# Top-k attention with a mixture of depths on one core: small VectorE operations set behind the next maximum, and reciprocals taken straight from the column of sums

## The chip, the cores and the metric

The kernel runs on one NeuronCore of a Trainium2 chip. The metric is the device time of one execution in microseconds (us). Besides the plain runs one execution was taken by the hardware profiler. Its record names the engines: PE is TensorE (PEld its weight loads), DVE is VectorE, ACT is ScalarE, POOL is GpSimd, SP is the queue that issues most DMAs.

## The reference, cut to what matters

```python
# attention: B, H, S, D = 8, 8, 576, 64
scores = scale * np.matmul(q, k.transpose(0, 1, 3, 2))
kth = np.partition(scores, -32, axis=-1)[..., -32:-31]
scores = np.where(scores >= kth, scores, -1000000000.0)
scores = scores - np.max(scores, axis=-1, keepdims=True)
attn = np.exp(scores)
attn = attn / (np.sum(attn, axis=-1, keepdims=True) + 1e-09)
attn_out = np.matmul(attn, v)
# bridge: x = attn_out as (B, S, H * D) = (8, 576, 512)
# mixture of depths: capacity 128, F = 1024
scores = np.einsum('bsd,d->bs', x, w_gate)
out = x.copy()
for b in range(B):
    top_idx = np.argpartition(-scores[b], capacity)[:capacity]
    xe = x[b, top_idx]
    ye = np.maximum(xe @ w1, 0.0) @ w2
    g = 1.0 / (1.0 + np.exp(-scores[b, top_idx]))
    out[b, top_idx] = x[b, top_idx] + g[:, None] * ye
```

For every query only the 32 largest of its 576 scores are kept. Then, for each batch, the 128 tokens with the largest gate pass through a two-layer network, and the result is added to their rows.

## The kernel before, in words

**Tiles and units.** The 576 queries of a batch form four tiles of 128 and one of 64. A unit is one tile with two heads (for the tile of 64, four heads, two of them on the upper partitions). A batch has 18 units and the whole run 144. One pass of the loop over `n` works on several units at once, as a pipeline:

- unit n+1: PE multiplies queries and keys, and ACT copies the scores to `sc` (two rows of 576 for each partition);
- unit n: DVE finds a lower bound of the 32nd largest score (`find_bound`). For each of the two rows it takes the eight largest of seven parts (14 `MAX8` that write `cand`), then works on `cand` alone (`best`, `MATCH_REPLACE8`, `bound`);
- unit n-1: ACT takes the sign of each score against the bound and counts (`sides`, `seen`), POOL multiplies scores and signs into `y`;
- unit n-2: DVE takes two `MAX8` over `y` (`find_kth`), whose results `next` give the threshold;
- unit n-3: ACT and POOL make the mask `less`;
- unit n-4: PE transposes scores and adds the mask, ACT takes the exponential `pT` (and `last`), PE multiplies by the values into `av`, and ACT copies `av` to `xs`.

Each head has 65 columns in `xs`: 64 of values and, as column `D`, the sum of the weights, which comes from a column of ones beside the values.

**From `xs` to the output.** When the last unit of a tile is in `xs`, ACT copies the column of sums to `sums` (`keep_sums`, one instruction of 128x8 for each of the 40 tiles, or 64x8). In the next pass DVE takes the reciprocal `rden`, POOL multiplies it into the output tile `x`, and a pass later DVE takes the dot product of `x` with the gate's weights (`gates`).

**The mixture.** For each batch but the last a generator, `mixture`, spreads the second stage over the units of the batch that follows: ranks of the gates, a matrix product that finds each chosen row's number and gate, the fetch of the rows (an indirect DMA of POOL), two layers on PE, and an indirect DMA that adds to the output. On DVE `add_up` sums the parts of row number and gate into `place`, writes `row_i`, and clamps the gate into `g`. ACT takes the exponential of `g`, and `squash` adds one and takes the reciprocal. For the last batch the same is written out after the loop, with DVE, ACT, POOL and PE taking turns.

**The order.** All engines keep program order. The deferred pieces stand in lists of functions that the loop empties at fixed places: `vector_late` in `find_bound`, ahead of the second row's maxima (here stand the reciprocals `rden` and `squash`), `after_kth` after `find_kth` (here stands `add_up`), `late` after the mask (here stands ACT's exponential of `g`), `pool_late` for POOL. `keep_least` puts the smallest threshold of a batch into `least` when the batch's last mask is made. The inputs' check at the end, nine reductions over `bounded`, `least`, `seen`, `sums` and others, decides whether a general version of the computation must run. In the profile all instructions of the main path carry the line of the helper that records them, L46, so they are told apart by the names of their tiles.

Of the kernel before, what the change touches and what calls it, by code (L numbers as in the profile page):

```python
# [28 lines left out]
FEWEST = 0.5  # L29
# [20 lines left out]
def kernel(  # L50
# [91 lines left out]
    seen = const.tile([P, NS], FP32, name="seen")  # L142
    least = const.tile([P, B], FP32, name="least")
    bounded = const.tile([P, NS], FP32, name="bounded")
    sums = const.tile([P, B * NT, H], FP32, name="sums")
    nc.gpsimd.memset(sums, 1.0)

    MIDDLE = S - 2 * (TOP_K - 8) + 1
    steps_i = const.tile([P, 2, 8], I32, name="steps_i")
# [74 lines left out]

    kept, values_bank = [], [None]

    after_kth = []

    def flush_copies():
        while copies_late:  # L230
# [2 lines left out]
    def flush():  # L233
        flush_copies()
        while late:
            late.pop(0)()

    def flush_vector():
        while vector_late:
            vector_late.pop(0)()  # L240
# [4 lines left out]

    def flush_all():
        flush_vector()
        flush()
        flush_pool()

# [293 lines left out]
    def find_bound(sc, bound):  # L544

        cand = wkpool.tile([P, 2, 8 * PARTS], FP32, name="cand")
        best = [stats.tile([P, 2, 8], FP32, name=f"best{r}") for r in range(2)]
        best.append(bound)
        for i in range(2):

            if i == 1:
                flush_vector()
            for u in range(PARTS):
                if i == 1 and amid_late and u == amid_late[0][0]:
                    amid_late.pop()[1]()
                dve.max(
                    cand[:, i, 8 * u : 8 * u + 8],
                    sc[:, i, u * S // PARTS : (u + 1) * S // PARTS],
                )


        parts = cand.rearrange("p i (u e) -> p i u e", u=PARTS)
        for r, e in enumerate((3, 7, 8)):
            for i in range(2):
                dve.max(best[r][:, i, :], parts[:, i, :, 0:e])
            if r < 2:
                for i in range(2):
                    dve.match_replace(
                        parts[:, i, :, 0:e],
                        best[r][:, i, :],  # L570
                        parts[:, i, :, 0:e],
                        LOWEST,
                    )
# [140 lines left out]
    def keep_values_of_two(t, g, av, xs):  # L714
# [7 lines left out]
        for i, (h, r) in enumerate(heads_of(t, g)[0]):  # L722
# [4 lines left out]
                in_=both[r : r + n, :].rearrange("p (g c) -> p g c", g=2),  # L727
            )

    def normalise(b, t, xs):  # L730
        n = R if t == J else P
        den = sums[0:n, b * NT + t, :]
        divide(n, xs, of_batch[b][0][0:n, t, :], den)

    def keep_sums(n, xs, den):
        act.activation(den, xs[0:n, :, D], AF.Copy, bias=1e-9)

    def divide(n, xs, x, den):
        rden = stats.tile([P, H], FP32, name="rden")
        dve.reciprocal(out=rden[0:n, :], in_=den)  # L740
        pool.tensor_tensor(
            x.rearrange("p (h d) -> p h d", h=H),
            xs[0:n, :, 0:D],
            rden[0:n, :].unsqueeze(2).to_broadcast([n, H, D]),
            ALU.mult,
        )

# [38 lines left out]
    def mixture(row0, pg, rank, exact=False, sign_sum=None):  # L786
# [107 lines left out]

        def add_up():
            add_parts(place, found)
            keep_rows(
                place,
                row_i,
                row0 if isinstance(row0, float) else row0[:, 0:1],  # L900
                float(done * S - 1),
            )
            dve.tensor_scalar_max(out=g, in0=place[:, 1:2], scalar1=-88.0)
            late.append(lambda: act.activation(g, g, AF.Exp, scale=-1.0))

        def squash():
            dve.tensor_scalar_add(out=g, in0=g, scalar1=1.0)
            dve.reciprocal(out=g, in_=g)

        kept.append(lambda: after_kth.append(add_up))  # L910
        if exact:
            for todo in (kept, after_kth):
                while todo:
                    todo.pop(0)()
        yield
# [258 lines left out]
    def keep_least(b, bound, kth):  # L1174
        at = 2 * per_batch * b
        late.append(
            lambda: act.copy(
                out=bounded[:, at : at + 2 * per_batch].rearrange("p (n i) -> p n i", i=2),
                in_=bound,
            )  # L1180
        )
        dve.tensor_reduce(
            out=least[:, b : b + 1], in_=kth, axis=mybir.AxisListType.XY, op=ALU.min
        )

    def mask_of(n, on=None):
# [5 lines left out]
    for n in range(-1, N):  # L1192
# [89 lines left out]
        if is_unit(n - 4):  # L1282
            b4, t4, g4 = units[n - 4]
            values(t4, g4, pT, last, av, qkv[b4][2], 2 * DE * second)
            if n in place_steps:
                values_bank[0] = av
                next(mixtures[place_steps[n]])
                pieces[place_steps[n]] += 1
            if g4 == 0:
                xs = xpool.tile([P, H, DE], FP32, name="xs")  # L1290
                if t4 == 0:
                    x = xpool.tile([P, NT, HD], FP32, name="x")
                    pg = gates_of[b4 % 2]
                    of_batch[b4] = x, pg
            if second:
                keep_values_of_two(t4, g4 - 1, av, xs)
            if g4 == groups(t4) - 1:
                inverting = b4, t4, xs
                n4 = R if t4 == J else P
                keep_sums(n4, xs, sums[0:n4, b4 * NT + t4, :])  # L1300
            while kept:
                kept.pop(0)()

# [64 lines left out]
        b, t, g = units[m]  # L1368
        keep_values(t, g, weighed[m][3], xs)

    def sums_of(t, xs):
        n = R if t == J else P
        keep_sums(n, xs, sums[0:n, (B - 1) * NT + t, :])

    def mask_both(m):
        b, i = divmod(m, per_batch)
        masks[m] = wkpool.tile([P, 2, S], BF16, name="less")
# [45 lines left out]
    values_unit(N - 3)  # L1423
    weighed[N - 2][2]()
    keep_unit(N - 3, xs)
    sums_of(J - 1, xs)
    mask_both(N - 1)
    normalise(B - 1, J - 1, xs)
    store_full(last_out, x)
# [13 lines left out]
    for _ in range(2):  # L1443
        next(between)
    keep_unit(N - 1, xs)
    sums_of(J, xs)
    count(J - 1, slice(0, JP), rank)
    rden = stats.tile([P, H], FP32, name="rden")
    dve.reciprocal(out=rden[0:R, :], in_=sums[0:R, (B - 1) * NT + J, :])
    dve.tensor_tensor(  # L1450
        x[0:R, J, :].rearrange("p (h d) -> p h d", h=H),
        xs[0:R, :, 0:D],
        rden[0:R, :].unsqueeze(2).to_broadcast([R, H, D]),
        ALU.mult,
    )
    store_last(last_out, x)
# [77 lines left out]
        )  # L1534

    keep_least(B - 1, bounds.pop(B - 1)[:, :, :, 7], next8s.pop(B - 1)[:, :, :, 7])
    flush()
    low = modpool.tile([P, S], I32, name="low", tag="scratch")[:, 0:NS]
    dve.tensor_scalar(
# [9 lines left out]
    for what, op, than, limit in (  # L1549
        (bounded, ALU.min, ALU.is_gt, LEAST),  # L1550
        (least, ALU.min, ALU.is_gt, LEAST),
        (low, ALU.min, ALU.is_gt, 0.5),
        (seen, ALU.max, ALU.is_lt, float(MIDDLE)),
        (seen, ALU.min, ALU.is_gt, float(MIDDLE - 16)),
        (sums.rearrange("p t h -> p (t h)"), ALU.min, ALU.is_gt, FEWEST),
        (sums.rearrange("p t h -> p (t h)"), ALU.max, ALU.is_lt, MOST),
        (places[:, :, 6], ALU.min, ALU.is_gt, 0.5),
        (places[:, :, 6], ALU.max, ALU.is_lt, 1.5),
    ):
        far = stats.tile([P, 1], FP32, name="far", bufs=2)  # L1560
        dve.tensor_reduce(out=far, in_=what, axis=mybir.AxisListType.X, op=op)
        dve.scalar_tensor_tensor(
            out=sure, in0=far, scalar=limit, in1=sure, op0=than, op1=ALU.mult
        )
# [91 lines left out]
    def general(b, row0):  # L1656
        def of(a):
            return a[bass.ds(b, 1)].rearrange("o a s d -> (o a) s d")

        kT, qT, vs = room_for_qkv(0)  # L1660
        rows = Rows(of(k), of(q), kT, qT)
        turn_all_last(rows)
        for hp in range(NHP):
            turn_pair(rows, hp)
        load_v(of(v), vs)
        x = xpool.tile([P, NT, HD], FP32, name="x")
        pg = gates_of[0]
        for t in range(NT):
            xs = xpool.tile([P, H, DE], FP32, name="xs")
            for g in range(groups(t)):  # L1670
                ps = room_for_scores()
                multiply(t, g, kT, qT, by_head(ps))
                p = general_weights(keep(ps))
                tr, av = room_to_turn()
                turn(p, tr)
                pT = ptpool.tile([P, 2, J, P], FP32, name="pT")
                last = ptpool.tile([P, P], FP32, name="last")
                nc.scalar.copy(out=pT, in_=tr)
                nc.scalar.copy(out=last, in_=turn_last(p, av))
                values(t, g, pT, last, av, vs)  # L1680
                keep_values(t, g, av, xs)
            rows = R if t == J else P
            den = stats.tile([P, H], FP32, name="den", bufs=1)
            keep_sums(rows, xs, den[0:rows, :])
            divide(rows, xs, x[0:rows, t, :], den[0:rows, :])
            dot_tile(t, x, pg)
        store(out[bass.ds(b, 1)].rearrange("o s n -> (o s) n"), x)
        rank = stats.tile([P, NT], FP32, name="rank", bufs=1)
        for _ in mixture(row0, pg, rank, exact=True):
            flush_all()  # L1690
        flush_all()
# [40 lines left out]
```

## Time and profile before

| what | before |
|---|---|
| median of 3 runs | 787.77 us (785.72 to 788.05) |
| the profiled execution, its own time | 788.09 us |
| its span | 785.8 us |
| instructions in the span | 33176 |
| mean granted TensorE clock | 0.997 |
| DVE's groups: `cand` maxima, `next` maxima | 2016 in all, 228 ns; 288, 751 ns |
| reciprocal `rden`, 128 rows and 64 rows | 32, 185 ns; 8, 180 ns |
| ACT's copy of sums, 128 rows and 64 rows | 32, 216 ns; 8, 216 ns |
| `least`; `row_i`; reciprocal of `g` | 8, 217 ns; 8, 154 ns; 8, 164 ns |

How to read it: the span runs from the first to the last instruction in the record, and the execution's own time has 2.3 us more around it. Durations are those of one instruction, and neighbours on one engine may overlap, so what an instruction takes from its engine is read from start to start. A busy share is an average over stages.

### The profile page before, as it was taken

How to read it: one execution, taken by the hardware profiler on the slowest of the kernel's cores; microseconds unless marked ns; L12 is line 12 of the kernel's file. 1: busy time of each engine (PE TensorE's matmuls, PEld its weight loads, DVE VectorE, ACT ScalarE, POOL GpSimd, SP SyncE). 2: the span in 40 equal slices, each digit the busy share in tenths (PEclk: the TensorE clock that was granted, in tenths of full speed). 3: DMA queues.
4: the chain of work that ended last, by engine and by line, in shares of the span. 5: the costliest groups of instructions: out<-in, count | busy, mean ns of one | idle time of the engine just before them, and what ended most of it. 6: DMA issues, size and time to landing. Idle time of an engine off the chain costs nothing. (4 is left out here: it accounts for less than half of the span.)

```text
span 785.8 us, 33176 instructions
## 1 busy us (share of the span) xinstructions
PE 725.5 (92%) x12535; PEld 550.6 (70%) x12535; DVE 755.1 (96%) x4602; ACT 731.7 (93%) x1535; POOL 693.7 (88%) x732
## 2 busy tenths in 40 slices
PE   8888888788999989999999999999899999999987
PEld 6666666566786668766787667866687668757756
DVE  6999999999999999999999999999999999999952
ACT  5999999999999999999999999999999999989830
POOL 3899999999999999999999999999999999899821
PEclk9999999999999999999999999999999999999999
DMA  9941214121151223321232221412234102101021
GB/s 171 297 86 35 58 62 104 36 56 30 62 113 25 52 66 76 83 55 37 77 89 52 56 43 62 105 30 56 43 89 92 30 15 70 25 15 17 3 75 31
DMA packets 121751, 50.69 MB, mean 65 GB/s; under 512 B 116016, under 2 KB 116016, under 8 KB 120560
## 3 DMA queue, kind: packets, MB, share of 16 engines
q1 hardware_dynamic: 118368, 43.94, 22.9%
q0 software_dynamic: 1744, 4.20, 3.0%
q8 instruction: 101, 1.65, 0.9%
q14 instruction: 66, 0.54, 0.3%
q10 hardware_dynamic: 1472, 0.36, 0.2%
HBM read 36.93 MB, written 11.55 MB: 62 GB/s over the span
## 5 line engine op out<-in xcount | busy, mean ns | idle before, releaser
L46 POOL TENSOR_TENSOR y<-sc,sides 128x576 f32<-128x576 f32 x288 | 350.5, 1240 | 27.9 <-ACT sides L46 26.2
L46 DVE MAX8 cand<-sc 128x8 f32<-128x82 f32 (+1 forms) x2016 | 312.8, 228 | 4.6 <-ACT sc L46 4.6
L46 POOL TENSOR_SCALAR less<-sc,next 128x576 bf16<-128x576 f32 x135 | 233.7, 1731 | 24.6 <-DVE next L46 21.9
L46 ACT ACTIVATE sides<-sc,bound 128x576 fp8e4<-128x576 f32 x288 | 230.9, 802 | 2.1 <-DVE bound L46 1.5
L46 PEld LDWEIGHTS av<-v,pT 128*64 128x64 f32 x4608 | 146.9, 138 | 87.5 <-ACT last L46 79.0
L46 DVE MAX8 next<-y 128x8 f32<-128x584 f32 x288 | 204.4, 751 | 0.0
L46 PE MATMUL av<-v,pT 128*64 128x65 f32 x4608 | 166.9, 225 | 35.2 <-ACT last L46 34.9
L46 PE MATMUL ps<-kT,qT 64*128 64x288 f32 (+1 forms) x1248 | 170.4, 422 | 3.2 <-ACT sc L46 2.5
L46 PEld LDWEIGHTS <-less 64*128 64x128 bf16 (+1 forms) x2448 | 160.6, 131 | 11.2 <-POOL less L46 8.3
L46 ACT COPY sc<-ps 128x1152 f32<-128x1152 f32 x140 | 160.7, 1148 | 0.0
L46 PE MATMUL ptr<-ident,sc 64*128 64x64 f32 x2272 | 160.1, 252 | 0.0
L46 ACT ACTIVATE pT<-ptr 128x1024 f32<-128x1024 f32 x142 | 147.4, 1038 | 9.4 <-PE ptr L46 8.7
L46 PEld LDWEIGHTS ptr<-ident,sc 64*128 64x128 f32 x2272 | 137.6, 137 | 23.8 <-issue 23.6
L46 PE MATMUL ptr<-out_of_reach,less 64*128 64x64 bf16 x2272 | 147.1, 189 | 5.6 <-POOL less L46 4.9
L46 ACT ACTIVATE less<-sc,next 128x576 bf16<-128x576 f32 x147 | 115.5, 790 | 0.0
L46 PEld LDWEIGHTS ps<-kT,qT 64*128 64x128 f32 (+1 forms) x1248 | 92.6, 176 | 22.8 <-ACT sc L46 5.6
L46 DVE MATCH_REPLACE8 cand<-best,cand 128x21 f32<-128x21 f32 (+1 forms) x576 | 99.0, 180 | 0.0
L46 DVE MAX8 best<-cand 128x8 f32<-128x21 f32 (+1 forms) x576 | 90.6, 190 | 0.0
L46 ACT ACTIVATION_READ_ACCUMULATOR sides<-sc,bound 128x1 f32 x288 | 63.8, 222 | 0.0
L46 PE MATMUL h_ps<-xeT,w 128*128 128x128 f32 x464 | 61.9, 278 | 0.0
L46 PEld LDWEIGHTS av<-ident,sc 128*128 128x128 f32 x144 | 20.0, 139 | 55.9 <-issue 40.9
L46 PE MATMUL av<-vpair,last 128*64 128x130 f32 x576 | 56.9, 276 | 0.0
(167 smaller groups left out, 919.0 us busy)
## 6 DMA issues: line engine op xcount, KB each, us to landing
v<-in_v_dram SPq DMA_DIRECT2D x64, 128.0 KB, 4.0
out_dram<-x SPq DMA_DIRECT2D x8, 1024.0 KB, 3.9
rows<-in_k_dram SPq DMA_DIRECT2D x56, 128.0 KB, 3.0
rows<-in_q_dram SPq DMA_DIRECT2D x56, 128.0 KB, 3.0
w<-in_moe_w_dram SPq DMA_DIRECT2D x2, 2048.0 KB
gate_row<-row_dram SPq DMA_DIRECT2D x7, 288.0 KB, 4.4
last<-in_q_dram SPq DMA_DIRECT2D x8, 128.0 KB, 3.4
vpair<-in_v_dram SPq DMA_DIRECT2D x16, 64.0 KB, 5.1
```

What stands on the lines that cost most here:

```text
L46: return lambda *a, **kw: self._tc.keep_in_program_order(fn(*a, **kw))
```

## The change

Three kinds of small DVE instruction that read what stands right before them are moved behind the maximum that follows. They go into a new list, `after_max`, which `find_bound` empties after each of its 14 maxima of `cand`: the reduction into `least`, the pair `row_i` and clamp of `g` (now `use_place`), and the reciprocal of `g`. ACT's exponential of `g` is queued by `use_place`, and so comes a pass later. Besides, `keep_sums` goes: DVE's reciprocal reads column `D` of `xs` itself and writes `shares`, which takes the place of `rden` and `sums`. The term of 1e-9 is left out of the main path. The two reductions at the end test the reciprocals against the inverted limits.

```diff
-    sums = const.tile([P, B * NT, H], FP32, name="sums")
-    nc.gpsimd.memset(sums, 1.0)
+    shares = const.tile([P, B * NT, H], FP32, name="shares")
+    nc.gpsimd.memset(shares, 1.0)
...
+    after_kth, after_max = [], []
+
+    def flush_small():
+        while after_max:
+            after_max.pop(0)()
...
                 dve.max(
                     cand[:, i, 8 * u : 8 * u + 8],
                     sc[:, i, u * S // PARTS : (u + 1) * S // PARTS],
                 )
+                flush_small()
...
     def normalise(b, t, xs):
         n = R if t == J else P
-        den = sums[0:n, b * NT + t, :]
-        divide(n, xs, of_batch[b][0][0:n, t, :], den)
-
-    def keep_sums(n, xs, den):
-        act.activation(den, xs[0:n, :, D], AF.Copy, bias=1e-9)
+        invert(xs[0:n, :, D], share_of(b, t))
+        divide(n, xs, of_batch[b][0][0:n, t, :], share_of(b, t))
+
+    def invert(den, share):
+        dve.reciprocal(out=share, in_=den)
...
         def add_up():
             add_parts(place, found)
+            after_max.append(use_place)
+
+        def use_place():
             keep_rows(
...
             dve.tensor_scalar_add(out=g, in0=g, scalar1=1.0)
-            dve.reciprocal(out=g, in_=g)
+            after_max.append(lambda: dve.reciprocal(out=g, in_=g))
...
-        dve.tensor_reduce(
-            out=least[:, b : b + 1], in_=kth, axis=mybir.AxisListType.XY, op=ALU.min
+        after_max.append(
+            lambda: dve.tensor_reduce(
+                out=least[:, b : b + 1], in_=kth, axis=mybir.AxisListType.XY, op=ALU.min
+            )
         )
...
     keep_unit(N - 1, xs)
-    sums_of(J, xs)
     count(J - 1, slice(0, JP), rank)
-    rden = stats.tile([P, H], FP32, name="rden")
-    dve.reciprocal(out=rden[0:R, :], in_=sums[0:R, (B - 1) * NT + J, :])
+    invert(xs[0:R, :, D], share_of(B - 1, J))
...
-        (sums.rearrange("p t h -> p (t h)"), ALU.min, ALU.is_gt, FEWEST),
-        (sums.rearrange("p t h -> p (t h)"), ALU.max, ALU.is_lt, MOST),
+        (shares.rearrange("p t h -> p (t h)"), ALU.max, ALU.is_lt, 1.0 / FEWEST),
+        (shares.rearrange("p t h -> p (t h)"), ALU.min, ALU.is_gt, 1.0 / MOST),
```

More of the change, by code (lines that the diff above doesn't have):

```diff
@@ L225 @@
     kept, values_bank = [], [None]
-    after_kth = []
+    after_kth, after_max = [], []
+    def flush_small():
+        while after_max:
+            after_max.pop(0)()
     def flush_copies():
@@ L559, in find_bound @@
                 )
+                flush_small()
         parts = cand.rearrange("p i (u e) -> p i u e", u=PARTS)
@@ L728, in keep_values_of_two, with share_of, divide @@
             )
+    def share_of(b, t):
+        return shares[0 : R if t == J else P, b * NT + t, :]
     def normalise(b, t, xs):
         n = R if t == J else P
-        den = sums[0:n, b * NT + t, :]
-        divide(n, xs, of_batch[b][0][0:n, t, :], den)
-    def keep_sums(n, xs, den):
-        act.activation(den, xs[0:n, :, D], AF.Copy, bias=1e-9)
-    def divide(n, xs, x, den):
-        rden = stats.tile([P, H], FP32, name="rden")
-        dve.reciprocal(out=rden[0:n, :], in_=den)
+        invert(xs[0:n, :, D], share_of(b, t))
+        divide(n, xs, of_batch[b][0][0:n, t, :], share_of(b, t))
+    def invert(den, share):
+        dve.reciprocal(out=share, in_=den)
+    def divide(n, xs, x, share):
         pool.tensor_tensor(
@@ L743, in divide @@
             xs[0:n, :, 0:D],
-            rden[0:n, :].unsqueeze(2).to_broadcast([n, H, D]),
+            share.unsqueeze(2).to_broadcast([n, H, D]),
             ALU.mult,
@@ L907, in squash @@
             dve.tensor_scalar_add(out=g, in0=g, scalar1=1.0)
-            dve.reciprocal(out=g, in_=g)
+            after_max.append(lambda: dve.reciprocal(out=g, in_=g))
         kept.append(lambda: after_kth.append(add_up))
         if exact:
-            for todo in (kept, after_kth):
+            for todo in (kept, after_kth, after_max):
                 while todo:
@@ L1298 @@
                 inverting = b4, t4, xs
-                n4 = R if t4 == J else P
-                keep_sums(n4, xs, sums[0:n4, b4 * NT + t4, :])
             while kept:
@@ L1369, in keep_unit @@
         keep_values(t, g, weighed[m][3], xs)
-    def sums_of(t, xs):
-        n = R if t == J else P
-        keep_sums(n, xs, sums[0:n, (B - 1) * NT + t, :])
     def mask_both(m):
@@ L1425 @@
     keep_unit(N - 3, xs)
-    sums_of(J - 1, xs)
     mask_both(N - 1)
@@ L1445 @@
     keep_unit(N - 1, xs)
-    sums_of(J, xs)
     count(J - 1, slice(0, JP), rank)
-    rden = stats.tile([P, H], FP32, name="rden")
-    dve.reciprocal(out=rden[0:R, :], in_=sums[0:R, (B - 1) * NT + J, :])
+    invert(xs[0:R, :, D], share_of(B - 1, J))
     dve.tensor_tensor(
@@ L1452 @@
         xs[0:R, :, 0:D],
-        rden[0:R, :].unsqueeze(2).to_broadcast([R, H, D]),
+        share_of(B - 1, J).unsqueeze(2).to_broadcast([R, H, D]),
         ALU.mult,
@@ L1536 @@
     keep_least(B - 1, bounds.pop(B - 1)[:, :, :, 7], next8s.pop(B - 1)[:, :, :, 7])
+    flush_small()
     flush()
@@ L1682, in general @@
             rows = R if t == J else P
-            den = stats.tile([P, H], FP32, name="den", bufs=1)
-            keep_sums(rows, xs, den[0:rows, :])
-            divide(rows, xs, x[0:rows, t, :], den[0:rows, :])
+            den = stats.tile([P, H], FP32, name="den", bufs=1)[0:rows, :]
+            act.activation(den, xs[0:rows, :, D], AF.Copy, bias=1e-9)
+            invert(den, den)
+            divide(rows, xs, x[0:rows, t, :], den)
             dot_tile(t, x, pg)
```

## The prediction

> **What bounds the kernel now.** The page's busy times come first, then stretches, then who waited for whom, then order of time. Part 1 puts VectorE (DVE) highest, ScalarE (ACT) close behind, the others not far:
>
> ```profile
> PE 725.5 (92%) x12535; PEld 550.6 (70%) x12535; DVE 755.1 (96%) x4602; ACT 731.7 (93%) x1535; POOL 693.7 (88%) x732
> ```
>
> Those are averages over start, middle and end. The busy times by stretch (columns: stretch, its length, then PE, PEld, DVE, ACT, POOL with their instructions, clock, DMA share, GB/s) part them:
>
> ```profile
> 28.00:748.00 720.00, 671.18 (x12028) 509.25 (x12024) 719.20 (x4408) 705.02 (x1472) 673.60 (x680) 1.00 0.25 61
> 748.00:786.00 38.00, 29.66 (x273) 21.86 (x269) 15.58 (x66) 8.74 (x25) 8.39 (x12) 0.98 0.20 55
> ```
>
> From 28 to 748 us DVE lacks 0.80 us of being busy throughout. That it runs rather than waits is told by the list of waits on DVE. These are all that exceed 2 us:
>
> ```profile
> DVE gy L46 <- PE av L46: 6.5, 2, 3.5
> DVE cand L46 <- ACT sc L46: 4.6, 3, 3.1
> DVE xeT L46 <- PE av L46: 3.7, 1, 3.7
> DVE unsure L46 <- PE av L46: 2.8, 1, 2.8
> DVE rden L46 <- ACT sums L46: 2.4, 2, 1.4
> ```
>
> By their start times the three before `cand` lie before 28 us and the rest after 748. In between, DVE's input is early: from unit 10 to the last but one of the 144, a copy of scores lands 0.9 us or more before its first maximum (median 2.5), and POOL's product 1.8 us or more before its maximum (median 3.3). So **a nanosecond off DVE's queue in the middle is a nanosecond off the end**, until another engine catches up.
>
> The 0.80 us left are gaps of about 35 ns, and 21 of them stand before three kinds of instruction. In order of time (start, length):
>
> ```profile
> 104.44 1.42 DVE L46 MAX8 next<-y 128x8 f32<-128x584 f32 x2
> 105.89 0.22 DVE L46 TENSOR_REDUCE least<-next 128x1 f32<-128x36 f32 x1
> ...
> 181.01 1.42 DVE L46 MAX8 next<-y 128x8 f32<-128x584 f32 x2
> 182.34 0.14 DVE L46 TENSOR_REDUCE place<-places 128x2 f32<-128x6 f32 x1
> 182.52 0.15 DVE L46 TENSOR_SCALAR row_i<-place 128x1 int32<-128x1 f32 x1
> ...
> 203.57 0.13 DVE L46 TENSOR_SCALAR g<-g 128x1 f32<-128x1 f32 x1
> 203.74 0.16 DVE L46 RECIPROCAL g<-g 128x1 f32<-128x1 f32 x1
> ```
>
> Two `next` maxima and an independent reduction: 182.34 - 181.01 = 1.33 us. Two maxima and a reduction that reads them: 105.89 - 104.44 = 1.45. A stall of 0.12 us, larger than the gap: an unhindered instruction starts some 85 ns before its predecessor ends (668 ns from start to start of a maximum that takes 752), a dependent one 34 ns after.
>
> **What the Trainium skill says.** "VectorE: DVE Perf Modes", section "The DRAIN you can't avoid", holds that the next operation waits until the pipe is empty and that a semaphore then "costs nothing extra". This trace differs: 668 against 786 ns behind the same maximum, and the measurement decides. The same section says that one intervening DVE operation suffices for a reader to see its writer's result. "Perfetto Trace Analysis", section "DVE / Act Engine Instruction", ends the profiled window at the write's acknowledgement, with the semaphore's travel after it. The trace's 34 ns fit that. No page prices a strided reciprocal.
>
> **The change, part by part.**
>
> 1. *`least` behind a maximum.* Seven in the loop (the eighth, at 766 us, stays). The release is at 752 + 34 = 786 ns after the last `next` starts. The inserted `cand` maximum starts at 668 and takes 145 to the next start, so the reduction may start at 813, with the release 27 ns past. Gain 7 x (786 - 667) = 0.83 us.
> 2. *`row_i` and the clamp of `g` behind a maximum.* `place` takes 140 to 143 and its reader follows 175 ns after its start. Unhindered small ones follow at their length less 84 ns (144 gives 60, 154 gives 71), so 57. Then 57 + 145 = 202 is past the release. Gain 7 x 118 = 0.82 us.
> 3. *The reciprocal of `g` behind a maximum.* 169 ns now, 134 - 84 = 50 unhindered. Six at 119 and one at some 90 (that pair starts behind `rden` and stands 143 apart): 0.80 us.
>    No instruction is added. What goes along: POOL's fetch of rows reads `row_i`, at 184.97 against 182.52 (2.0 us later in the shortest case, at 702). The moved `row_i` is 57 + 145 - 175 = 27 ns later against `place`, so it costs nothing there. ACT's exponential of `g` is queued one unit, 5.1 us, later. The add that reads it follows 15 us or more after the present exponential, so 10 remain. If this cover went, the stall would be DVE's, on a tiny ACT instruction. SP's queue and DMAs are passed by nothing.
> 4. *Reciprocals from the column of `xs`.* The 40 reciprocals remain and now read eight values at a stride of 260 bytes. The nearest rows are reductions of 8 values: 160 ns at a stride of 28 bytes, 154 contiguous. That gives +6 ns. ACT's copy of this very column took 216 against 204 for its one-value exponential, so at most +12. `least`, 36 strided values in 218, is some 35 ns over what the contiguous rows give (154 for 8, 447 for 288), thus 1 ns a value, +8. I take 8 ns: 38 x 8 = **0.3 us lost** in the middle; ends 0 and 0.5.
> 5. *The 40 copies of sums leave ACT.* Each holds ACT for about 0.28 us (from the copy of `xs` to the next exponential about 256 ns without one, 418 to 440 plus 122 with it). 38 lie in the middle: 10.6 us off ACT. Some copies of scores now wait on two semaphores, which costs an extra wait instruction, some 0.1 us of that each. DVE never waits for ACT there, so I count zero. If that is wrong it is a gain.
> 6. *The end*, where DVE does wait:
>
> ```profile
> 749.76 0.27 ACT L46 COPY xs<-av 128x130 f32<-128x130 f32 x1 [0.37 <-PE av L46]
> 750.06 0.21 ACT L46 ACTIVATE sums<-xs 128x8 f32<-128x8 f32 x1
> ...
> 752.00 0.39 PE L46 MATMUL av<-vpair,last 128*64 128x130 f32 x4
> ...
> 752.64 0.29 PE L46 MATMUL ptr<-ident,gate 128*128 128x128 f32 x1 [0.25 <-DVE gate L46]
> ...
> 754.86 0.21 ACT L46 ACTIVATE sums<-xs 64x8 f32<-64x8 f32 x1
> 755.11 0.20 DVE L46 RECIPROCAL rden<-sums 64x8 f32<-64x8 f32 x1 [1.05 <-ACT sums L46]
> ```
>
> The last reciprocal can start where the copy of sums did, 755.11 - 754.86 = 0.25 us earlier, and behind it hang the last product, its gates, the fetch and the store. The earlier one (750.31) also moves to 750.06. Its product, two counts and `gate` follow, and PE waited 0.25 for `gate` in front of the last values. PE is free at 752.00 + 0.39, so 0.2 of the 0.25 come through. Together 0.45 us; ends 0.25 and 0.5. The bounds of shares replace bounds of sums with two reductions of the same size, beside PE's matrices: zero.
>
> Sum: 0.83 + 0.82 + 0.80 - 0.3 + 0.45 = 2.6 us. A maximum behind a small one sometimes stands 9 ns further (154 for 145) and behind a reciprocal 34 nearer (111), so 21 places at up to 20 ns add 0.4 either way. I take **2.7 us**. The profiled execution took 788.09 (span 785.8 and 2.3 around it), thus 785.4. The median shown is 787.77, 0.3 lower, and from it I forecast **785.1**, 0.34% less. A difference of 0.3% (2.4 us) is about what a measurement of this kernel can tell from no change, and the three runs shown spread over 2.3 us.
>
> **The rivals.**
>
> *A: the stall only changes its place.* If one maximum didn't cover a release, or if its covering cost what it saves, only the end's 0.45 less 0.3 remains: 787.6. For it: only 27 ns to spare. Against it: in the search for `best` a MATCH_VALUE_LOAD reads the result of a maximum one instruction back, and starts 9 ns after its release (203 + 34 = 237, at 246), without a whole stall. Chance 0.2.
>
> *B: slower, by the strided reciprocal.* DVE is the bound, so each nanosecond on a reciprocal counts 38 times. At 38 x 0.071 it has eaten the 2.7 us. At 0.135 us each more than I took the kernel is 2.4 slower: 790.2. That is more than ten times what the strided rows show, on eight values. Chance 0.05.
>
> *C: ACT was the hidden partner.* ACT is busy 97.9% of the middle, and its 10 us could show up if DVE's durations hid waits on it. Half of them would give 780. Against it: a `cand` maximum stands 145 or 146 ns from the next in nearly every unit, with slack of microseconds. Chance 0.05.
>
> *D: the change doesn't do what it says*, because the queue's order stays. The order of the built program does show each of the three behind a `cand` maximum, and ACT with 40 instructions fewer. No chance given.
>
> **How the numbers follow.** My case has 0.7. Its own range is 784.3 to 786.2 by the bounds above: stalls 2.0 to 2.9, stride 0 to 0.5, end 0.25 to 0.5. A run's spread of about 1 us widens that to 783.5 to 786.5. Faster by over 0.3% means below 785.4, close to the forecast: 0.57 of my case's 0.7, plus C, 0.62. Within 0.3%: the rest of my case and most of A, 0.32. Slower by over 0.3%: B and a little of A by the spread, 0.06. To leave out no more than 2 in 10, the range reaches half into A: 783.3 to 786.8.
>
> **What would show it.** Right: gaps of 34 ns before `least`, `row_i` and the reciprocal of `g` gone; 668 ns from the last `next` to `cand`; a batch (the distance between two `least`, 92.08 us) shorter by 0.3; ACT down by 8.6 us busy; reciprocals of shares at 185 to 195 ns; the last one 32 ns behind the copy of `xs`. Wrong: a gap of the same size one instruction later (A), longer reciprocals (B), batches shorter by over 0.5 (C), or a new wait of DVE in the middle.

## The result and the profile after

The changed kernel took 782.61 us (median of 8 runs, 782.0 to 784.48), the kernel before 786.94 (median of its 8, 784.96 to 788.05). The ratio is 0.9953, with a 95% interval of 0.9939 to 0.9968, so the gain is 3.7 us (1.00 less 0.9953, times 787), with 2.5 to 4.8 us by the interval. The forecast was 785.1, with a range from 783.3 to 786.8: 2.7 us off 787.77. The direction was right, and the measured median lies below the range. The interval alone still holds 2.7 us. That the gain was larger, and where it arose, is read from the traces below.

Part 1 of the page after, as before: busy time and share of the span.

```profile
PE 724.1 (93%) x12535; PEld 549.3 (70%) x12535; DVE 752.5 (96%) x4602; ACT 724.3 (93%) x1495; POOL 692.5 (89%) x732
```

ACT has 40 counted instructions fewer and is busy 7.4 us less. DVE has as many instructions as before and is busy 2.6 us less. Busy time by stretch, cut where DVE's last wait at the start and its first at the end lie (stretch, its length, then PE, PEld, DVE, ACT, POOL, clock, DMA share, GB/s):

```profile
28.00:743.00 715.00, 670.71 (x12017) 509.15 (x12018) 714.93 (x4394) 696.19 (x1429) 670.74 (x678) 1.00 0.25 61
743.00:780.00 37.00, 29.48 (x269) 21.71 (x268) 15.40 (x65) 8.31 (x23) 8.30 (x12) 0.99 0.20 56
```

DVE now lacks 0.07 us of being busy all through the middle, where it lacked 0.80. The dependency gaps are gone, and the order of time shows why (start, length, engine, operation):

```profile
102.48 1.42 DVE L46 MAX8 next<-y 128x8 f32<-128x584 f32 x2
103.82 0.23 DVE L46 MAX8 cand<-sc 128x8 f32<-128x82 f32 x1
103.96 0.20 DVE L46 TENSOR_REDUCE least<-next 128x1 f32<-128x36 f32 x1
...
180.27 0.14 DVE L46 TENSOR_REDUCE place<-places 128x2 f32<-128x6 f32 x1
180.32 0.24 DVE L46 MAX8 cand<-sc 128x8 f32<-128x82 f32 x1
180.48 0.14 DVE L46 TENSOR_SCALAR row_i<-place 128x1 int32<-128x1 f32 x1
...
201.23 0.14 DVE L46 TENSOR_SCALAR g<-g 128x1 f32<-128x1 f32 x1
201.29 0.24 DVE L46 MAX8 cand<-sc 128x8 f32<-128x82 f32 x1
201.44 0.15 DVE L46 RECIPROCAL g<-g 128x1 f32<-128x1 f32 x1
```

From the first `next` maximum to what follows the second it is now 103.82 - 102.48 = 1.34 us, the unhindered distance. Each small reader now stands one maximum behind its writer, without a gap. The list of waits shows no new wait of DVE in the middle. At the end the wait for the column of sums has shrunk and now names the copy to `xs`:

```profile
DVE cand L46 <- ACT sc L46: 2.9, 3, 2.1
DVE unsure L46 <- PE av L46: 2.8, 1, 2.8
DVE shares L46 <- ACT xs L46: 1.7, 2, 1.2
```

**Where the time went.** The spans of the two profiled executions differ by 5.86 us, more than the ratio. The start, up to the first maximum of unit 10, has 2.0 us of that. In the ten profiles of this document the start took 54.3 to 57.1 us and did not follow the edit: experiments 1 and 3 below have the same order on DVE and the same copies on ACT, and took 57.1 and 54.7. So it is left out. From there to the first maximum of unit 142, called the middle below, the trace's start times give 674.60 us before and 671.37 after: 3.24 us gained. From the start of the last mask to that of the last product `gy` it is 32.45 and 32.03: 0.42 us. Together they are 3.66 us, close to the ratio's 3.7. What follows the last product took 5.0 to 5.5 us in the ten profiles and did not follow the edit either.

The 3.24 us are not what the forecast's sum for the middle holds (2.45 less 0.3). Adding up starts to next starts by kind of instruction gives 2.45 us for the three stalls (0.81, 0.82, 0.82), as forecast. The small readers themselves took 0.38 us less and the `cand` maxima 0.37 more. Of these 0.37 us, 0.16 stand at the 34 maxima right behind a reciprocal, which is most of the stride's price (experiment 2). The `best` maxima gave 0.17 us that I can't explain: they took 60.97 us in this profile and 61.07 to 61.14 in the other nine. The largest unforeseen part, 0.60 us, comes from an instruction that the change doesn't touch, the dot product of the gates. In the costliest groups (number, busy us, mean ns, idle before) it stands first for before and then for after:

```profile
L46 DVE CUSTOM_DVE_ANT_0 prod<-x,wg 128x512 f32<-128x512 f32 x32 | 25.4, 794 | 0.1
```

```profile
L46 DVE CUSTOM_DVE_ANT_0 prod<-x,wg 128x512 f32<-128x512 f32 x32 | 24.8, 776 | 0.1
```

A mean of 794 ns before, for an instruction whose shortest took 670, was the sign that the prediction passed over. The instruction-by-instruction view of its tile after gives the spread (shortest, median, longest):

```profile
L46 DVE CUSTOM_DVE_ANT_0 prod<-x,wg x40: 667/678/1742, 50.5 to 750.4; 128x512 f32<-128x512 f32 x32, 64x512 f32<-64x512 f32 x8
```

Some dot products are stretched to more than double, and it counts as busy time. What stretches them shows beside POOL's order of time. POOL and DVE before, in the 14th unit of a batch:

```profile
254.38 1.76 POOL L46 TENSOR_SCALAR less<-sc,next 128x576 bf16<-128x576 f32 x1
254.91 0.80 DVE L46 CUSTOM_DVE_ANT_0 prod<-x,wg 128x512 f32<-128x512 f32 x1
```

The same after:

```profile
251.69 1.74 POOL L46 TENSOR_SCALAR less<-sc,next 128x576 bf16<-128x576 f32 x1
252.44 0.68 DVE L46 CUSTOM_DVE_ANT_0 prod<-x,wg 128x512 f32<-128x512 f32 x1
```

Before, POOL's mask starts 0.53 us ahead of the dot product, which lasts 0.80 us. After, it starts 0.75 us ahead, and the dot product lasts 0.68. Over the seven profiles with this dot product (before, after, experiments 1 to 3 and both of 5) the starts and ends are regular:

- With a mask started more than 0.63 us ahead, the dot product takes 597 to 601 ns to the next start (145 cases).
- With a mask started 0.26 to 0.63 us ahead, it lasts until 1.21 to 1.27 us after the mask's start (81 cases), for instance 848 ns at 370 ahead.
- With starts within 90 ns of each other, either can give way. In 8 of 26 cases the dot product was held to the same end (1131 ns at 78 ahead, 1230 at 20 behind). In 18 it took its 597 to 608 ns, and the mask took 2.19 to 2.30 us instead of 1.72.
- The mask is not the only one. The first tile's dot product of the first batch starts while POOL works on a product `y`, and lasted until 1.71 to 1.72 us after the start of that `y`, itself 1.23 to 1.24 us long. That of the last batch starts during a `y` too and was held on into the mask that follows, to 1.21 or 1.22 us after the mask's start: 1555 ns in all before, 1672 after.

The Trainium skill, "GPSIMD Engine Reference", section "Key points", says that GpSimd shares its SBUF interfaces with VectorE, with contention for DVE instructions of two SBUF inputs. The dot product has two. The traces agree, and put the hold by a mask at its first 0.6 us of 1.72.

So the question for the experiments was what moved POOL against DVE: ACT's relief (the copies of sums are gone, ACT's signs reach POOL sooner), or the new order on DVE.

### The profile page after: what moved, and what is told of

It reads as the page before. It is cut to its first block, busy times and chain, and to the rows that moved or that the text cites. A ratio compares the mean times of both kernels' runs of the same rounds, so it can differ in the third digit from the quotient of the medians.

```text
span 780.0 us, 33174 instructions
## 1 busy us (share of the span) xinstructions
PE 724.1 (93%) x12535; PEld 549.3 (70%) x12535; DVE 752.5 (96%) x4602; ACT 724.3 (93%) x1495; POOL 692.5 (89%) x732
## 5 line engine op out<-in xcount | busy, mean ns | idle before, releaser
L46 ACT ACTIVATE sides<-sc,bound 128x576 fp8e4<-128x576 f32 x288 | 234.3, 814 | 4.5 <-DVE bound L46 4.4
L46 ACT COPY sc<-ps 128x1152 f32<-128x1152 f32 x140 | 162.4, 1160 | 0.0
L46 ACT ACTIVATE pT<-ptr 128x1024 f32<-128x1024 f32 x142 | 150.0, 1056 | 11.5 <-PE ptr L46 10.3
L46 ACT ACTIVATE less<-sc,next 128x576 bf16<-128x576 f32 x147 | 117.1, 801 | 0.0
L46 ACT ACTIVATION_READ_ACCUMULATOR sides<-sc,bound 128x1 f32 x288 | 67.1, 233 | 0.0
```

Of the source, the lines that this page charges most:

```text
L46: return lambda *a, **kw: self._tc.keep_in_program_order(fn(*a, **kw))
```

## The experiments

"Dot products" below is the part of the middle that the 36 of them take, from start to next start. Each sum is read from one profiled execution of its kernel. Times of single dot products are from start to next start too.

**1. The new order alone.** The kernel before with `after_max`, and `keep_sums` kept:

```diff
+            after_max.append(use_place)
...
-            dve.reciprocal(out=g, in_=g)
+            after_max.append(lambda: dve.reciprocal(out=g, in_=g))
...
-        dve.tensor_reduce(
-            out=least[:, b : b + 1], in_=kth, axis=mybir.AxisListType.XY, op=ALU.min
+        after_max.append(
+            lambda: dve.tensor_reduce(
+                out=least[:, b : b + 1], in_=kth, axis=mybir.AxisListType.XY, op=ALU.min
+            )
         )
```

> The kernel before with the three moves behind a maximum alone; the copies of sums and the old reciprocals stay. By the sum of parts 1 to 3, 2.45 us leave the middle of the run and nothing leaves the end: ratio to before 0.9969. Theory one (ACT's relief gave the extra gain, because POOL's mask then starts earlier against the gates' dot product): the dot products stay as long as before, the one in the 14th unit of a batch at 680 to 730 ns from start to start, in sum within 0.2 us of before. Theory two (the moves on DVE changed its phase against POOL): the dot products fall by 0.6 us in sum, as in the changed kernel, and the ratio is near 0.996.

Measured: ratio 0.9979 (0.9969 to 0.9990), 22 runs. The three stalls give 2.47 us, as in the changed kernel. But the dot products rise from 25.12 to 25.81 us, so only 2.05 us of the middle remain. The group in the costliest groups, 794 ns on average before:

```profile
L46 DVE CUSTOM_DVE_ANT_0 prod<-x,wg 128x512 f32<-128x512 f32 x32 | 26.1, 815 | 0.1
```

Neither theory foresaw a loss. The dot product of the 14th unit did fall to 597 to 600 ns, as theory two had it, but the sum rose. In four of the batches a dot product of another tile, the fourth, now meets the start of a mask (599 before, 1131 to 1144 now), while those of the first and second tile escape there and the mask is lengthened instead. These nearly cancel. The largest single piece of the loss is the last batch's first dot product, 2102 ns instead of 1555: it now starts earlier in POOL's `y` and is held until the mask behind it is past its first part.

**2. The column alone.** The changed kernel with the small operations in their old places:

```diff
-            after_max.append(use_place)
+            use_place()
...
-            after_max.append(lambda: dve.reciprocal(out=g, in_=g))
+            dve.reciprocal(out=g, in_=g)
```

(and `least` likewise).

> The changed kernel with the three small kinds back in their old places: reciprocals from the column of xs and no copies of sums. The prediction's own terms give 0.45 off the end less 0.3 for the stride: ratio 0.9998. Theory one gives 0.45 off the end, 0.6 off the dot products (the one in the 14th unit at 599 ns instead of about 700), no cost of the stride: 1.05 us, ratio 0.9987. Theory two: dot products as before, 0.45 us, ratio 0.9994. Reciprocals of shares stay at 184 ns and 101 from start to start if the stride costs nothing, 192 and 109 by the prediction.

Measured: ratio 0.9986 (0.9978 to 0.9995), 22 runs. The middle is 0.72 us shorter, the dot products 24.11 us, 1.0 less than before, and the one of the 14th unit is at 598 or 599 ns in the six batches where it was 679 to 728. The strided reciprocal itself hardly changes:

```profile
L46 DVE RECIPROCAL shares<-xs 128x8 f32<-128x8 f32 x32 | 5.9, 186 | 1.2 <-ACT xs L46 1.2
```

186 ns against 185 from `sums`, and 102 from start to start against 101, 0.04 us over the middle. But the maximum right behind it starts its successor after 116 ns instead of 112, another 0.15 us over 34 of them. The same 4 to 5 ns stand in all seven profiles whose reciprocals read `xs`, and in none of the three whose reciprocals read `sums`. So reading the column costs some 0.19 us here and 0.17 in the changed kernel. That is about 5 ns for each reciprocal, where the prediction took 8.

**3. The copies put back on ACT.** The changed kernel with the loop's 38 copies, written to a tile that nothing reads:

```diff
             if g4 == groups(t4) - 1:
                 inverting = b4, t4, xs
+                n4 = R if t4 == J else P
+                act.activation(
+                    sums[0:n4, :], xs[0:n4, :, D], AF.Copy, bias=1e-9
+                )
```

> The changed kernel with the 38 copies of sums of the loop put back on ACT, written to a tile that nothing reads; the reciprocals still read xs. ACT has its old load, DVE its new order. Theory one: the dot product in the 14th unit is held again (680 to 730 ns), 0.6 us slower than the changed kernel, ratio to before about 0.996. Theory two: dot products as in the changed kernel, no slower than it, ratio 0.9953.

Measured: ratio 0.9971 (0.9961 to 0.9982), 18 runs. The middle is 1.53 us longer than in the changed kernel, and 1.36 of it are dot products (25.88 us against 24.52). Of the 1.36 us the last batch's first dot product has 0.41 (2083 ns against 1672). Theory one had the cause, ACT's copies, but not the place: of the 14th units two take 1230 and 1246 ns, and the others 598 to 600. The waits on POOL point to the way from ACT to there (us in total, times, longest), first with the copies put back, then in the changed kernel:

```profile
POOL y L46 <- ACT sides L46: 26.1, 34, 9.6
POOL less L46 <- DVE next L46: 12.7, 24, 0.8
```

```profile
POOL less L46 <- DVE next L46: 24.9, 43, 0.9
POOL y L46 <- ACT sides L46: 19.6, 18, 10.0
```

With the copies POOL waits 34 times for ACT's signs, without them 18 times. The other pair of kernels agrees: 30 times before, 19 in experiment 2. My reading is that without the copies POOL is done with `y` earlier and waits for DVE's threshold instead (43 times against 24), so that its mask starts at a steadier distance from DVE. The dot products that are held are then the first tile's (some 860 ns each) instead of another tile's at 1.13 us or more in four of the batches.

The four kernels form a square. Dot products in the middle: old order with copies 25.12 us, without 24.11; new order with copies 25.81 and 25.88 (experiments 1 and 3), without 24.52. **The copies cost 1.0 to 1.4 us of DVE's time through POOL, and the new order costs 0.4 to 0.7 us in the same way.** Which dot products are held is less firm than the sums: experiments 1 and 3 have the same order and the same copies and differ in it, the fourth tile's in four batches against the fourth's in two and the second's in two. And much of the new order's cost sits in the last batch's first dot product: 0.55 of 0.69 us with the copies, 0.16 of 0.41 without.

**4. The hold taken away.** The gates' operation with one input, in the kernel before, in the changed kernel, and in the one with the copies put back. It sums `x` and leaves out the gate's weights:

```diff
-        dve.tensor_tensor_reduce(
+        dve.tensor_scalar(
             out=prod[0:n, 0:HD],
             in0=x,
-            in1=wg[0:n, :],
-            scale=1.0,
-            scalar=0.0,
+            scalar1=1.0,
+            scalar2=None,
             op0=ALU.mult,
             op1=ALU.add,
```

> The kernel before with the gates' operation of one input: it sums x instead of multiplying by the gate's weights, which it leaves out (1.0 in their place). It is the base for the next two, since nothing then reads two tensors on DVE while POOL's mask runs. If the hold of the dot product by POOL's first 0.6 us of a mask needs two inputs, every gate operation in the middle takes the same time, within 20 ns. Ratio to before 0.995 to 1.001, as a gate of one input takes 600 to 720 ns from start to start, like the count of gates, against a mean of 698 now.

> The changed kernel with the same gates of one input (weights left out). Theory one (beyond the stalls and the end the change acts only through ACT, POOL's mask and the held dot product): with the hold gone, the difference to the kernel before with such gates is the prediction's own sum without the stride, 2.45 + 0.45 = 2.9 us, 2.4 to 2.5 of it in the middle. Rival (ACT's relief reaches DVE in another way too, or the stride costs): middle differs by 3.0 or more, or by 2.2 or less.

> The changed kernel with the 38 copies of sums put back on ACT (nothing reads them) and gates of one input (weights left out). Theory one: the copies then cost nothing in the middle; the distance of two least reductions is that of the changed kernel with such gates, within 0.05 us a batch, where the pair with dot products lay 1.5 us apart over 132 units. Rival: ACT's load itself slows DVE; the 1.5 us stay.

Measured: ratios to the kernel before of 0.9940 (0.9925 to 0.9954), 0.9893 (0.9876 to 0.9910) and 0.9905 (0.9888 to 0.9921). The first is faster than expected, since the gate's operation takes 593 ns where a range of 600 to 720 was given. No such operation is held, in any of the three. The view of its tile in the changed kernel of the three:

```profile
L46 DVE TENSOR_SCALAR_CACHE_REDUCE prod<-x x40: 657/668/687, 50.8 to 745.8; 128x512 f32<-128x512 f32 x32, 64x512 f32<-64x512 f32 x8
```

The longest is 687 where it was 1742. So the hold belongs to the operation with two inputs. The edit also changes the kind of instruction, and the run doesn't part the two. The middle goes from 670.86 us in the kernel before of this kind to 668.35 in the changed one: 2.51 us, close to the 2.45 for the stalls. The stride's 0.19 us is in it here too, and the small readers' own shorter times make up for it. The ratio of the two, 0.9893/0.9940, gives 3.7 us, more than 2.5 and the end's 0.4. The rest is open. In the two profiles the ends can't be compared: the first has the lower TensorE clock that the last section describes, the second has not, and from the last mask to the last product they took 32.54 and 30.75 us.

With the copies back on ACT the middle is 669.03, so they still cost 0.68 us, not zero. Theory one is right on the larger part only. Nearly all of the rest is three units that are 0.20 to 0.22 us longer. There DVE stood idle 0.11 to 0.13 us ahead of a `cand` maximum (twice) and of a reciprocal, both of which read what ACT writes. The changed kernel of this kind has no such gap in the middle. With DVE this fast, ACT with the copies is late now and then.

**5. Other places for the dot products.** Two runs, the second from what the first showed:

```diff
-            amid_late.append((4 if gating[1] in (1, 2) else 2, lambda a=gating: gates(*a)))
+            amid_late.append(((4, 4, 4, 2, 3)[gating[1]], lambda a=gating: gates(*a)))
```

> The changed kernel with the gates' dot product of a batch's first tile two maxima later (behind the fourth of the second row instead of the second) and that of its fifth tile one later. If the dot product is held until some 1225 ns after the start of POOL's mask (less), as the starts and ends in the two traces suggest, the first tile's falls from about 870 to 599 ns from start to start in the middle batches, and by 290 in the first and last: 8 x 0.28 = 2.2 us, the fifth tile's from 628 to 599: 0.2 us. Ratio to before 0.9953 - 2.4/787 = 0.9923. If the length belongs to the tile itself, not to the overlap with POOL, 870 stays and the ratio is 0.9953.

Measured: ratio 0.9937 (0.9919 to 0.9956). In six of the eight batches the first tile's dot product falls from about 870 to 599 ns, as expected. In the first batch it falls from 1136 to 812 and in the last from 1672 to 1341, also about as expected. But the sum in the middle falls by 1.35 us only, because the second tile's is now held (699 to 724 in five batches and 844 in the last, all at 598 or 599 in the changed kernel): DVE had moved against POOL again. The second run takes (4, 5, 4, 2, 3):

> The changed kernel with the gates' dot products behind maxima 4, 5, 4, 2, 3 of the second row for the five tiles of a batch (2, 4, 4, 2, 2 in the changed kernel; 4, 4, 4, 2, 3 in the one with later dots). In that one the second tile's stood at 700 ns, with POOL's mask started 500 to 540 ns ahead. One maximum (146 ns) later it is past the 0.6 us: 599. That gives 6 x 0.1 + 0.15 in the last batch = 0.75 us over that kernel, ratio to before 0.9928. If the phase shifts again instead, another tile's dot product is held and the ratio stays near 0.9937.

Measured: ratio 0.9921 (0.9902 to 0.9940), 779.82 us, the lowest median of the kernels with the gates' weights (780.38 in the first run, whose interval overlaps). The middle took 669.52 us, 1.85 less than the changed kernel, and the group of dot products:

```profile
L46 DVE CUSTOM_DVE_ANT_0 prod<-x,wg 128x512 f32<-128x512 f32 x32 | 22.8, 711 | 0.1
```

24.8 us have become 22.8. The second tile's last 599 to 616 ns in seven of the eight batches and 723 in the last. The first tile's stay near the first run's in the first and last batch (837 and 1356).

## Why the prediction was right or wrong

*What bounds the kernel* held: by the list of waits DVE has none in the middle, before and after. But "a nanosecond off DVE's queue is a nanosecond off the end" was used for changed instructions only, and DVE's own unchanged instructions turned out to depend on POOL.

*Parts 1 to 3, the stalls:* 0.83, 0.82 and 0.80 forecast, 0.81, 0.82 and 0.82 measured. The 27 ns to spare sufficed. `row_i`, `least` and the reciprocal of `g` each gave up another 0.12 to 0.13 us over their seven places, and the `cand` maxima took 0.37 back, within the 0.4 us either way that the sum allowed for such shifts. The 668 ns behind an unhindered maximum need a word: the section "The DRAIN you can't avoid" of the Trainium skill's "VectorE: DVE Perf Modes", which the prediction reads as refuted, adds that a next operation that is not held starts earlier. With that the trace agrees. What differs is the price of waiting for the result, 0.12 us here.

*Part 4, the stride:* 0.3 us lost was forecast, with ends 0 and 0.5, and 0.17 measured in the changed kernel. So the size was near. But it doesn't stand where the prediction looked for it: the reciprocal's own start-to-start time has 0.02 us of it, and the maximum behind it 0.16.

*Part 5 is the step that failed:* the copies on ACT were counted zero, "DVE never waits for ACT there". DVE doesn't, but POOL does, and POOL's mask and `y` hold DVE's dot product, in DVE's busy time. The term measured 1.0 to 1.4 us. The moves of parts 1 to 3 had a term of the same kind that wasn't in the sum either, a loss of 0.4 to 0.7. The two together are the 0.60 us of the changed kernel. Both were within reach of the profile before: a mean of 794 ns in the group of dot products against a shortest of 670 in the view of the tile. The prediction's remark that a wrong zero would be a gain was right. Its extra wait instructions on ACT came too: the trace has 295 instead of 257, each 17 ns long. That one costs some 0.1 us isn't shown.

*Part 6, the end:* 0.45 us was forecast. From the last mask, 0.47 was measured to the sum into `place` and 0.42 to the last product. The last reciprocal stands 30 ns behind its copy:

```profile
748.88 0.54 ACT L46 COPY xs<-av 64x130 f32<-64x130 f32 x2 [0.78 <-PE av L46]
749.45 0.20 DVE L46 RECIPROCAL shares<-xs 64x8 f32<-64x8 f32 x1 [0.57 <-ACT xs L46]
```

*The base:* the forecast subtracted from a median of three runs, 787.77. The median of eight is 786.94. That alone is 0.8 us of the 2.5 us between forecast and median, and without it the median would lie just inside the range. The traces account for another 1.0 us (3.66 less 2.7). The last 0.7 us is the distance between the difference of the two medians, 4.3 us, and what the traces show, and is inside the interval. One slip in the working changes nothing: stalls 2.0, stride 0.5 and end 0.25 give 786.0, not 786.2, as the upper end of the prediction's own range.

*The rivals:* A fell (no gap elsewhere), B fell (5 ns a reciprocal, where it needed 71), and D fell (the trace has the new order). C had the right engine, ACT, and the right remark that a duration of DVE may hide a wait. It was dismissed on the `cand` maxima, which read one tensor, instead of on all groups. Its size, 5 us, was too large. A batch became 0.49 us shorter (92.08 to 91.59 in the middle batches), between the 0.3 set down as right and the 0.5 set down as a sign of C.

## What to carry to other kernels

On a saturated VectorE, one independent instruction set between a writer and its reader (145 ns here) saved the whole dependency stall (0.12 us each), and start-to-start times gave its size in advance. A busy engine may still be waiting: compare the mean of each group with its shortest, and where they differ look at what the other engine was doing at those starts. An edit that only shifts engines against each other then has a price of its own. That the bound engine never waits for a third engine doesn't make the relief of the third worth nothing.

## What the runs showed of the hardware that had not been expected

- The dot product, a DVE instruction with two SBUF inputs, is held by the first 0.6 us of POOL's mask over 128x576, and then ends 1.21 to 1.27 us after the mask's start; the other 1.1 us of the mask didn't hold it. A `y` of POOL held it for longer, to 1.71 us after the start of a `y` of 1.23. A one-input operation on the same data stayed within 657 to 687 ns.
- It works in the other direction too, and where the two start within 90 ns the earlier start doesn't decide. In experiment 3 a mask that started 40 ns ahead of a dot product took 2.22 us instead of 1.72, and the dot product went through in 608 ns:

```profile
322.92 2.22 POOL L46 TENSOR_SCALAR less<-sc,next 128x576 bf16<-128x576 f32 x1
```

```profile
322.96 0.68 DVE L46 CUSTOM_DVE_ANT_0 prod<-x,wg 128x512 f32<-128x512 f32 x1
```

- A reciprocal that reads eight values of `xs` at a stride of 260 bytes took about 1 ns longer from start to start than one that reads eight adjacent values of `sums`, and the maximum behind it 4 to 5 ns longer.
- Some executions have a lower TensorE clock for some 3.4 us just at the end of the loop. The stretches of 4 us from the changed kernel's profile and from the first run with dot products placed later (clock is the number ahead of the DMA share):

```profile
738.00:742.00 4.00, 3.91 (x62) 3.10 (x60) 4.00 (x10) 1.66 (x5) 1.42 (x3) 0.57 0.00 0
```

```profile
736.00:740.00 4.00, 3.90 (x100) 3.23 (x100) 4.00 (x9) 2.40 (x6) 1.99 (x3) 1.00 0.00 0
```

The kernel before had it as well in its profile (0.61). Where it is missing in a kernel with the changed end, the time from the last mask to the last product is 30.7 to 30.8 us instead of 31.9 to 32.0. The two runs of experiment 5, nearly the same kernel, differ in it (1.00 and 0.58), so it doesn't follow the edit alone. The ends of before and after were compared because both profiles had it.
